# Attention, token and channel mixing and a gated block on one core: another planner, and channel mixing that adds six blocks at once

## The chip, the core and the metric

One core of a Trainium2 chip runs the program. The metric is device microseconds of one execution. TensorE is called PE here, VectorE DVE, ScalarE ACT, GpSimd POOL; SyncE (SP) issues the DMAs.

## What is computed

Batch 4, sequence 448, model width 768 (12 heads of 64), all float32:

```python
scores = q @ k.T / 8 ; scores[upper triangle] = -1e9
attn = exp(scores - max) ; attn /= sum(attn) + 1e-9
x = attn @ v                                    # heads side by side: 448 x 768 a batch
u = x + (relu(x.T @ w_tok1) @ w_tok2).T         # token mixing, 448 -> 256 -> 448
y = u + relu(u @ w_ch1) @ w_ch2                 # channel mixing, 768 -> 1536 -> 768
h = relu(y @ w_in) ; a, v = halves of h         # 512 wide each
vn = (v - mean(v)) / sqrt(var(v) + 1e-6)
out = (a * (w_spatial @ vn + b_spatial)) @ w_out
```

## The kernel before

**Products.** Each float32 operand is split into a rounded part and a rest, and a product is three matmuls (`mm3`, L336 to L338). The left operand of a matmul is 128 x 128, the right one up to 448 columns.

**Attention.** There are 24 pairs of heads (pair n is batch n // 6). A pair's scores (PE, bank `pss`, L497) are made in two jobs, one for the row blocks 3 and 0 and one for 2 and 1; they use 64 of PE's rows for each head. DVE masks them and takes the maximum (L506), ACT takes the exponential (L523), POOL normalises (L544), the result is transposed (PE, `pst`, L581; in the last pairs on DVE), and a weighted sum follows (PE, `pso`, L683 and L688), which uses 64 of PE's columns for each head. All other matmuls use the whole array.

**Token mixing** of half a batch (`psm`) transposes U, multiplies twice, and DVE adds the result to U (L787).

**Channel mixing** of batches 0 and 1 is `channel(b)`: 24 units of weights of 128 x 768, in the order of `UNITS` (L32 to L34). A unit (1, f) is hidden block f: 18 matmuls into a bank `ps1`, relu on ACT (L843) and its rest on DVE (L330) into `hid`. There are six buffers `h0` to `h5`. A unit (2, q, e) holds the weights from the hidden blocks 3q to 3q+2 to two output blocks: for each output block 9 matmuls into a bank `ps2`, and DVE adds the bank to U (L859). That is 48 additions in the two batches. The units come as three of the first kind, then three of the first and three of the second in turn. Both kinds take the PSUM banks 6 and 7. Batches 2 and 3 use products that need fewer multiplications (`channel_pair`, bank `psf`; L1001 and L1080 are DVE's sums), and then comes the gated block (`psv`, `psf`, `psp`).

**Weights** arrive as 64-bit words. `narrow` (L343 to L358) makes float32 of a piece of 384 columns in three DVE steps, each of which reads what the one before wrote in a PSUM bank `psw`:

```python
if k == 0:   # L351
    nc.vector.tensor_scalar(o, words(1), 3, 0x3FFFFFFF, op0=ALU.logical_shift_left, op1=ALU.bitwise_and)
elif k == 1: # L353
    nc.vector.scalar_tensor_tensor(o, words(1), 0xC0000000, o, op0=ALU.bitwise_and, op1=ALU.bitwise_or)
else:        # L355
    nc.vector.scalar_tensor_tensor(w().bitcast(U32), words(0), 29, o, op0=ALU.logical_shift_right, op1=ALU.bitwise_or)
```

A unit is loaded into one of the buffers `way` (768 KB, L381), converted in two pieces, stored in DRAM as `plain` (384 KB, L395) and loaded again as `whl` (L818), where ACT and POOL split it (L819, L820 by way of L327). `whl` has four buffers. The weights of the gated block go the same way as `gw`. Pieces of the first eight units use bank 7, all later ones bank 3.

**The order of the work** is made by a planner. All work is recorded as jobs with an engine, a duration, what they read and write, and a priority. `Plan.order` (L~135 to L~200) runs a list scheduler (`run`) that goes through a model of the engines: of the jobs that could start first on an engine (within 0.03) the one with the lowest priority number is taken. Then `due` works backwards through that plan and gives every job its latest start as its priority. That is done up to six times, and the plan that ends first in the model is written out as each engine's program. An engine works through its program in order. The names and lines that the prediction speaks of are those above.

Of the kernel before, what the change touches and what calls it, by code (L numbers as in the profile page):

```python
# [2 lines left out]

# [59 lines left out]
PASSES = 6  # L63
DUE = "ACT", "DVE", "POOL", "SP", "PE"
# [9 lines left out]


class Buf:


    def __init__(self, make, tag, prev=None, banks=None):
        self.make, self.tag, self.prev, self.banks = make, tag, prev, banks  # L80
        self.jobs, self.tile, self.left = [], None, 0

# [7 lines left out]
class Job:  # L90
    def __init__(self, eng, us, emit, prio, at, size, index, port, other):
        self.eng, self.us, self.emit, self.prio, self.at, self.size, self.index = eng, us, emit, prio, at, size, index
        self.other = other
        self.port = port or eng == "POOL"
        self.before, self.after, self.bufs = set(), [], set()


class Plan:
# [11 lines left out]
    def job(self, eng, us, emit, r=(), w=(), touch=(), prio=0.0, at=0.0, size=0, port=False, other=None):  # L110


        j = Job(eng, us, emit, prio, at, size, len(self.jobs), port, other)
# [16 lines left out]
        j.bufs |= set(touch)  # L130
        self.jobs.append(j)
        return j

    def order(self):
# [10 lines left out]
        own = {j: (j.eng, j.us, j.emit, j.prio) for j in self.jobs}  # L145
        best = None
        for k in range(PASSES):
            for j in self.jobs:
                j.eng, j.us, j.emit, _ = own[j]
            if not self.run():  # L150
                break
            end = max(j.start + j.us for j in self.jobs)
            if best is None or end < best[0]:
                best = end, [(j.start, j.eng, j.us, j.emit) for j in self.jobs], {b: b.tag for j in self.jobs for b in j.bufs if b.banks}
            self.due(end, own, k)
        for j, x in zip(self.jobs, best[1]):
            j.start, j.eng, j.us, j.emit = x
        for b, tag in best[2].items():
            b.tag = tag
        return sorted(self.jobs, key=lambda j: (j.start, j.index))  # L160

    def due(self, end, own, k):

        jobs = sorted(self.jobs, key=lambda j: (j.start, j.index))
        owners = {}
        for j in jobs:
            for b in j.bufs:
                if b.banks and b not in owners.setdefault(b.tag, []):
                    owners[b.tag].append(b)
        later = {}  # L170
# [3 lines left out]
        late, pe = {}, end  # L174
        for j in reversed(jobs):
            t = pe if j.eng == "PE" else end
            for a in j.after:
                lat = 0.0
                if a.eng != j.eng or j.eng == "SP":
                    lat = 0.25 if j.eng == "PE" else 0.1  # L180
                    if a.eng == "PE":
                        lat += 0.3 if j.start < START else 0.8
                if j.eng == "SP":
                    lat += j.size / 340e3 + LANDING
                t = min(t, late.get(a, end) - lat)
            for b in j.bufs:
                if j in b.jobs:
                    for a in later.get(b, ()):
                        t = min(t, late.get(a, end) - 0.3)
            late[j] = t - j.us  # L190
            if j.eng == "PE":
                pe = late[j]
        for j in self.jobs:
            if own[j][0] in DUE and own[j][3] < 1e8:
                j.prio = late[j]

    def run(self):
# [11 lines left out]
        dma = port_free = 0.0  # L209
        avail = {e: [] for e in engines}  # L210
        def add(j):
            for e in (j.eng, j.other[0]) if j.other else (j.eng,):
                avail[e].append(j)

# [4 lines left out]
        def start(j, e):  # L219
            s = max(free[e], j.ready, port_free if j.port else 0.0)  # L220
            for b in j.bufs:
                if b.banks and b.tag is None:
                    s = max(s, min(bank_free[i] for i in b.banks))
            return s

        done = 0
        while done < len(self.jobs):
            best = None
            for e in engines:
                if not avail[e]:  # L230
                    continue
                starts = [(start(j, e), j) for j in avail[e]]
                first = min(s for s, _ in starts)
                if first == inf:
                    continue
                s, j = min(((s, j) for s, j in starts if s <= first + 0.03), key=lambda x: (x[1].prio, x[1].index))
# [4 lines left out]
            s, j, e = best  # L241
            avail[j.eng].remove(j)
            if j.other:
                avail[j.other[0]].remove(j)
                if e != j.eng:
                    j.eng, j.us, j.emit = j.other
            for b in j.bufs:
                if b.banks and b.tag is None:
                    b.tag = min(b.banks, key=lambda i: (bank_free[i] > s, -bank_free[i] if bank_free[i] <= s else bank_free[i]))
                    bank_free[b.tag] = inf  # L250
            j.start = s
            free[j.eng] = s + j.us
            if j.port:
                port_free = s + j.us
            end = s + j.us
# [4 lines left out]
            for b in j.bufs:  # L260
                if j in b.jobs:
                    b.left -= 1
                    if b.left == 0 and b.banks:
# [1244 lines left out]
```

## Time and profile before

| | before |
|---|---|
| runs, us | 759.65 (759.39 to 760.97), median of 3 |
| profiled execution: span, us | 760.7 |
| profiled execution: own time, us | 760.97, the highest of the three, is the nearest to its span |
| PE busy, us | 747.2 |
| DVE busy, us | 622.3 |
| ACT busy, us | 427.4 |
| POOL busy, us | 298.2 |
| DMA, MB | 122.0 |

Times in rows are microseconds from the start of the span. "Busy" is the time in which an engine worked on an instruction. A row of the timeline has the start, the length, engine, line and operation, the output and input by their names, and in brackets how long the engine was idle before it and which instruction ended the wait. Matmuls overlap, so their starts are to be compared, not their lengths. PEclk is the clock that PE was granted, as a share of 2.4 GHz.

### The profile page before, as it was taken

The numbers are of one execution on the slowest core, as the hardware profiler recorded it, in microseconds if no ns is written. First come the engines' busy times: TensorE is split into PE (matmuls) and PEld (weight loads), VectorE is DVE, ScalarE is ACT, GpSimd is POOL, SyncE is SP. The second block draws the span as 40 slices with busy tenths as digits, with TensorE's granted clock in tenths as the row PEclk, the third lists the DMA queues.
The fourth block names the chain that finished last, engine by engine and source line by source line (L and its number), as shares of the span: only waits on it lengthen the run. The fifth ranks groups of instructions, "written<-read, shape, count | busy, mean of one in ns | idle before, by whom it ended". The sixth has DMA issues, their size and how long they took to land. (4 is left out here: it accounts for less than half of the span.)

```text
span 760.7 us, 12440 instructions
## 1 busy us (share of the span) xinstructions
PE 747.2 (98%) x4216; PEld 640.3 (84%) x4216; DVE 622.3 (82%) x1512; ACT 427.4 (56%) x1040; POOL 298.2 (39%) x354
## 2 busy tenths in 40 slices
PE   8999999999989999999999999999999999999998
PEld 4577778888887888888889989998988888888997
DVE  6999599999867878876469978999999897599482
ACT  6998776445347765552336666654573665545241
POOL 4788764265494766563310000000420151542210
PEclk9999999999999999999999999999999999999999
DMA  6687158999976898898823122520301100400213
GB/s 228 207 285 238 55 163 316 335 318 333 339 225 190 298 307 250 234 304 220 241 84 117 39 84 84 187 84 1 118 22 42 43 0 1 132 1 28 83 49 133
DMA packets 48608, 122.02 MB, mean 160 GB/s; under 512 B 4896, under 2 KB 20256, under 8 KB 48032
## 3 DMA queue, kind: packets, MB, share of 16 engines
q1 hardware_dynamic: 48544, 121.23, 48.7%
q8 instruction: 33, 0.54, 0.3%
q14 instruction: 31, 0.25, 0.1%
HBM read 91.46 MB, written 29.75 MB: 159 GB/s over the span
## 5 line engine op out<-in xcount | busy, mean ns | idle before, releaser
L336 PE MATMUL psf<-fb,fa 128*128 128x448 f32 x420 | 154.0, 367 | 1.2 <-DVE hs L1001 0.6
L337 PE MATMUL psf<-fb,fa 128*128 128x448 f32 x420 | 153.7, 366 | 0.0
L338 PE MATMUL psf<-fb,fa 128*128 128x448 f32 x420 | 153.6, 366 | 0.0
L327 POOL TENSOR_TENSOR whl<-whl 128x768 fp32r<-128x768 f32 x45 | 83.2, 1851 | 89.5 <-ACT whl L819 89.4
L523 ACT ACTIVATE P<-P,stats 128x448 f32<-128x448 f32 (+3 forms) x192 | 96.1, 505 | 31.1 <-DVE stats L506 30.8
L544 POOL TENSOR_SCALAR P<-P,stats 128x448 f32<-128x448 f32 (+3 forms) x192 | 88.3, 483 | 38.1 <-DVE stats L535 30.8
L336 PEld LDWEIGHTS psf<-fb,fa 128*128 128x128 f32 x420 | 78.9, 188 | 9.2 <-DVE hs L1001 1.0
L337 PEld LDWEIGHTS psf<-fb,fa 128*128 128x128 f32 x420 | 78.9, 188 | 6.8
L338 PEld LDWEIGHTS psf<-fb,fa 128*128 128x128 f32 x420 | 78.9, 188 | 6.7
L506 DVE CUSTOM_DVE_ANT_0 P<-pss,mask 128x448 f32<-128x448 f32 (+3 forms) x192 | 70.9, 415 | 16.4 <-PE pss L497 16.0
L938 ACT CAST fa<-raw 128x384 fp32r<-128x384 f32 (+1 forms) x112 | 56.4, 531 | 42.7 <-DVE raw L951 21.6
L327 POOL TENSOR_TENSOR wv<-wf,wv 128x512 fp32r<-128x512 f32 x6 | 9.2, 1546 | 153.2 <-ACT wv L1156 153.2
L327 DVE TENSOR_TENSOR fa<-raw,fa 128x384 fp32r<-128x384 f32 (+1 forms) x109 | 61.0, 585 | 7.1 <-ACT fa L938 7.1
L336 PE MATMUL ps<-hid,whl 128*128 128x448 f32 x144 | 55.2, 383 | 3.1 <-DVE hid L330 1.9
L819 ACT CAST whl<-whl 128x768 fp32r<-128x768 f32 x45 | 37.4, 833 | 34.6 <-DMA whl<-plain 33.5
L336 PE MATMUL ps<-uhl,whl 128*128 128x448 f32 x144 | 55.6, 386 | 0.2 <-DVE U L859 0.2
L338 PE MATMUL ps<-hid,whl 128*128 128x448 f32 x144 | 53.3, 370 | 0.0
L337 PE MATMUL ps<-hid,whl 128*128 128x448 f32 x144 | 53.3, 370 | 0.0
L338 PE MATMUL ps<-uhl,whl 128*128 128x448 f32 x144 | 52.7, 366 | 0.0
L337 PE MATMUL ps<-uhl,whl 128*128 128x448 f32 x144 | 52.7, 366 | 0.0
L859 DVE TENSOR_TENSOR U<-ps,U 128x448 f32<-128x448 f32 x48 | 29.5, 619 | 20.9 <-PE ps L338 20.8
L327 POOL TENSOR_TENSOR ql<-stage,qh 128x896 fp32r<-128x896 f32 x18 | 38.1, 2116 | 14.9 <-issue 11.7
(174 smaller groups left out, 1793.2 us busy)
## 6 DMA issues: line engine op xcount, KB each, us to landing
way<-in_wch SPq DMA_DIRECT2D x24, 768.0 KB, 5.7
whl<-plain SPq DMA_DIRECT2D x45, 384.0 KB, 5.0
stage<-in_qkv SPq DMA_DIRECT2D x23, 448.0 KB, 4.7
plain<-way SPq DMA_DIRECT2D x24, 384.0 KB, 6.7
raw<-plain SPq DMA_DIRECT2D x24, 384.0 KB, 3.9
round<-PB SPq DMA_DIRECT2D x7, 1024.0 KB, 6.2
PT<-round SPq DMA_DIRECT2D x28, 256.0 KB, 6.2
v<-in_qkv SPq DMA_DIRECT2D x24, 256.0 KB, 4.1
```

The lines of the kernel that those rows point to most:

```text
L327: e.tensor_tensor(lo, x, hi.bitcast(F32), op=ALU.subtract)
L336: nc.tensor.matmul(ps, ah, bh, start=(first and i == 0), stop=False, **kw)
L337: nc.tensor.matmul(ps, ah, bl, start=False, stop=False, **kw)
L338: nc.tensor.matmul(ps, al, bh, start=False, stop=(last and i == n - 1), **kw)
L506: nc.vector.tensor_tensor_reduce(out=P(i)[:M, j, :], in0=ps(i, j), in1=mask[:M, S - 128 : S - 128 + W] if j == 0 and n < BLOCKS or M == 64 ...
L523: nc.scalar.activation(P(i)[:M, j, :], P(i)[:M, j, :], AF.Exp, bias=s.t[:M, 0, c : c + 1], scale=-1.0, accum_out=s.t[:M, 1, c : c + 1])
L544: nc.gpsimd.tensor_scalar(P(i)[:M, j, :], P(i)[:M, j, :], s.t[:M, 2, c : c + 1], 1.0, op0=ALU.mult, op1=ALU.mult)
L819: job("ACT", act(DM, False), lambda: nc.scalar.copy(w.t[:, 0, :], w.t[:, 1, :].bitcast(F32)), r=ks, w=ks, prio=p)
L859: job("DVE", dve(S), lambda d=d, ps=ps: nc.vector.tensor_tensor(u.t[:, d, :], ps.t[:, :S], u.t[:, d, :], op=ALU.add), r=[(ps, 0), *u_keys( ...
L938: job("ACT", act(n, False), lambda: nc.scalar.copy(part(o, 0), at(d)), r=[key(d)], w=[wk], prio=p + 0.1 * o)
```

## The change

Three things change. First, the planner. A job has a `mode` (1 for the scores, which tile PE's rows, 2 for the weighted sums, which tile its columns, 0 for all else); in the model a change of mode costs `SWITCH`, and a job in another mode than the last one has its priority number raised by `STAY`. A DVE job that reads what a DVE job wrote starts `CHAIN` later than that one ends. Durations of DVE and of some PE jobs are other numbers. Priorities come from two rules, `late` (as before) and `justified` (which packs each engine backwards), up to eight passes each, and then from 300 random variations of the best plan's priorities; the plan that ends first in the model is kept. Second, the units of channel mixing come as six of the first kind, then six of the second, twice, and an output block of batches 0 and 1 sums six hidden blocks, that is two units, 18 matmuls, in one bank before DVE adds it to U: 24 additions (L938) instead of 48. Third, the pieces of the first eight units may use bank 7 or bank 3.

The core of the diff (renamed helpers, the backward pass of `justified` and the caching in `run` are left out):

```diff
-UNITS = [(1, f) for f in range(3)]
-for q in range(4):
-    UNITS += [(1, f) for f in range(3 * q + 3, min(3 * q + 6, NF))] + [(2, q, e) for e in range(3)]
+UNITS = []
+for x in range(2):
+    UNITS += [(1, f) for f in range(6 * x, 6 * x + 6)] + [(2, q, e) for e in range(3) for q in (2 * x, 2 * x + 1)]
...
-PASSES = 6
+PASSES, TRIALS = 8, 300
+SWITCH, STAY, NEAR = 0.105, 3.0, 0.03
+CHAIN = 0.115
...
+        for rule in (self.late, self.justified):
+            prios = [j.own[3] for j in self.jobs]
+            for _ in range(PASSES):
+                if not self.attempt(prios):
+                    break
+                prios = rule(self.end)
+        dice = Random(1)
+        for _ in range(TRIALS):
+            spread, share = dice.choice((0.3, 1.0, 3.0)), dice.choice((0.02, 0.1, 0.5))
+            lo = dice.uniform(-50.0, 450.0) if dice.random() < 0.5 else None
+            hi = None if lo is None else lo + dice.choice((10.0, 30.0, 100.0))
+            prios = [p + dice.gauss(0.0, spread) if p < 1e7 and (lo is None or lo <= p < hi) and dice.random() < share else p for p in self.best[1]]
+            self.attempt(prios)
...
+            if e == "PE":
+                s, j = min(((s, j) for s, j in starts if s <= first + NEAR), key=lambda x: (x[1].prio + (x[1].mode != mode) * STAY, x[1].index))
+                return s + (j.mode != mode) * SWITCH, j
...
-        return (n * 1.05 + 60) / 1e3 if psum else (n * 1.09 + 40) / 1e3
+        return (n * 1.042 + 68) / 1e3
...
-            job("DVE", (n * 1.03 + 165) / 1e3, lambda k=k: step(k), r=[dk, (ps, 0)] if k else [dk], w=[wk] if k == 2 else [(ps, 0)], touch=[wk[0]], prio=prio)
+            job("DVE", (n * 1.04 + 70) / 1e3, lambda k=k: step(k), r=[dk, (ps, 0)] if k else [dk], w=[wk] if k == 2 else [(ps, 0)], touch=[wk[0]], prio=prio)
...
-        convert(i % 3 if i < 6 else 1 + i % 2, wch[:, i * DM : i * DM + DM], parts, LOW + i, (7,) if i < 8 else (3,), keep=i)
+        convert(i % 3 if i < 6 else 1 + i % 2, wch[:, i * DM : i * DM + DM], parts, LOW + i, (7, 3) if i < 8 else (3,), keep=i)
...
     def ch2(b, q, e, i):
-        w = WU[b, i]
+        w = [WU[b, i - 1], WU[b, i]]
         u = U[b]
-        hs = [hidden[b, 3 * q + f] for f in range(3)]
         for dd in range(2):
             d = 2 * e + dd
             ps = bank(banks_c, "ps2")
+            for x in range(2):
+                hs = [hidden[b, 3 * (q - 1 + x) + f] for f in range(3)]
+
+                def mms(dd=dd, ps=ps, x=x, hs=hs):
+                    cs = [slice(HALF * dd + 128 * f, HALF * dd + 128 * f + 128) for f in range(3)]
+                    mm3(ps.t[:, :S], [(w[x].t[:, 0, c], w[x].t[:, 1, c], h.t[:, 0, :], h.t[:, 1, :]) for c, h in zip(cs, hs)], first=x == 0, last=x == 1)
+
+                job("PE", 1.82, mms, ...)
             job("DVE", dve(S), lambda d=d, ps=ps: nc.vector.tensor_tensor(u.t[:, d, :], ps.t[:, :S], u.t[:, d, :], op=ALU.add), ...)
...
             if u[0] == 1:
                 ch1(b, u[1], i, xs)
-            else:
+            elif u[1] % 2:
                 ch2(b, u[1], u[2], i)
```

Every matmul of the program before is in the changed one. How the order moves is shown at three places. DVE in the channel mixing of batch 0, before: `psw` and `way` or `gw` rows are conversions, a `U` row is the addition of an output block.

```order
L859 TENSOR_TENSOR U_317<-ps_2478,U_317 128x448
L351 TENSOR_SCALAR psw<-gw 128x384
L353 SCALAR_TENSOR_TENSOR psw<-gw,psw 128x384
L355 SCALAR_TENSOR_TENSOR gw<-gw,psw 128x384
L859 TENSOR_TENSOR U_317<-ps_2500,U_317 128x448
L351 TENSOR_SCALAR psw<-way_156 128x384
L353 SCALAR_TENSOR_TENSOR psw<-way_156,psw 128x384
L355 SCALAR_TENSOR_TENSOR way_156<-way_156,psw 128x384
L859 TENSOR_TENSOR U_317<-ps_2519,U_317 128x448
```

The same place in the changed program:

```order
L429 TENSOR_SCALAR psw<-way_158 128x384
L938 TENSOR_TENSOR U_331<-ps_1580,U_331 128x448
L431 SCALAR_TENSOR_TENSOR psw<-way_158,psw 128x384
L433 SCALAR_TENSOR_TENSOR way_158<-way_158,psw 128x384
L938 TENSOR_TENSOR U_331<-ps_1620,U_331 128x448
L429 TENSOR_SCALAR psw<-way_158 128x384
L431 SCALAR_TENSOR_TENSOR psw<-way_158,psw 128x384
L433 SCALAR_TENSOR_TENSOR way_158<-way_158,psw 128x384
L429 TENSOR_SCALAR psw<-way_154 128x384
L431 SCALAR_TENSOR_TENSOR psw<-way_154,psw 128x384
L433 SCALAR_TENSOR_TENSOR way_154<-way_154,psw 128x384
```

Before, each addition had one piece's conversion ahead of it; now there are steps of up to three pieces between two additions, and an addition may stand between two steps of a piece.

PE in the early pairs, before: `pss` rows are scores, `pso` rows weighted sums, `psm` and `pst` rows use the whole array.

```order
L497 MATMUL pss<-ql,qh 64x64 x2
L497 MATMUL pss<-qh,ql 64x64 x2
L741 MATMUL psm<-ident,U_317 64x128 x3
L683 MATMUL pso<-PT,v 64x448 x2
L688 MATMUL pso<-PT,v 64x384 x2
L688 MATMUL pso<-PT,v 64x256 x2
L688 MATMUL pso<-PT,v 64x128 x2
L741 MATMUL psm<-ident,U_317 128x128 x3
L497 MATMUL pss<-qh 128x320 x2
L497 MATMUL pss<-ql,qh 128x320 x2
```

Pairs of the same batch in the changed program:

```order
L766 MATMUL pso<-PT,v 64x256 x2
L766 MATMUL pso<-PT,v 64x128 x2
L575 MATMUL pss<-qh 128x448 x2
L575 MATMUL pss<-ql,qh 128x448 x2
L575 MATMUL pss<-qh,ql 128x448 x2
L575 MATMUL pss<-qh 64x64 x2
L575 MATMUL pss<-ql,qh 64x64 x2
L575 MATMUL pss<-qh,ql 64x64 x2
L575 MATMUL pss<-qh 128x320 x2
L575 MATMUL pss<-ql,qh 128x320 x2
L575 MATMUL pss<-qh,ql 128x320 x2
```

Before, the two jobs of a pair's scores had whole-array work and a weighted sum between them; now they follow each other and the weighted sum directly. Counted over the whole program, PE goes from one of the three kinds to another 121 times before and 99 times now.

DVE at the start, before: `stats` and `P` rows are the reductions of the first pairs, `way` is a weight of token mixing.

```order
L534 TENSOR_SCALAR stats_65<-stats_65 128x4
L535 RECIPROCAL stats_65<-stats_65 128x4
L506 ISA P_208,stats_66<-pss,mask 128x448
L506 ISA stats_66 128x1
L534 TENSOR_SCALAR stats_65<-stats_65 128x4
L535 RECIPROCAL stats_65<-stats_65 128x4
L506 ISA P_208,stats_66<-pss,mask 128x448
```

The same place in the changed program:

```order
L612 TENSOR_SCALAR stats_65<-stats_65 128x4
L613 RECIPROCAL stats_65<-stats_65 128x4
L429 TENSOR_SCALAR psw<-way_152 128x384
L584 ISA P_211,stats_66<-pss,mask 128x448
L584 ISA stats_66 128x1
L612 TENSOR_SCALAR stats_65<-stats_65 128x4
L613 RECIPROCAL stats_65<-stats_65 128x4
L584 ISA P_211,stats_66<-pss,mask 128x320
```

The first step of the first conversion, which before came after all reductions of pair 1, now stands ahead of them.

## Rows read from the trace of the kernel before

**Rows 1.** The page's first part: busy time, share of the span, instructions of each engine.

```profile
PE 747.2 (98%) x4216; PEld 640.3 (84%) x4216; DVE 622.3 (82%) x1512; ACT 427.4 (56%) x1040; POOL 298.2 (39%) x354
```

**Rows 2.** Stretches of 20 us: busy time of each engine, PE's clock, DMA share, GB/s.

```profile
40.00:60.00 20.00, 19.93 (x154) 15.87 (x151) 19.01 (x51) 18.22 (x54) 18.06 (x29) 1.00 0.85 268
...
140.00:160.00 20.00, 20.00 (x115) 17.16 (x114) 19.15 (x41) 6.59 (x12) 5.54 (x3) 1.00 1.00 354
180.00:200.00 20.00, 18.68 (x96) 16.02 (x95) 18.39 (x44) 7.69 (x18) 8.07 (x7) 1.00 0.94 332
200.00:220.00 20.00, 18.07 (x84) 16.28 (x83) 14.49 (x31) 10.55 (x19) 14.90 (x15) 0.91 0.85 287
```

**Rows 3.** PE's waits: line, releaser, us in total, times, longest.

```profile
PE ps L336 <- DVE hid L330: 1.9, 1, 1.9
PE ps L336 <- DVE U L859: 1.2, 2, 1.1
PE psp L1355 <- DVE gate L1363: 0.9, 2, 0.7
PE psf L336 <- DVE hs L1001: 0.6, 1, 0.6
PE psf L336 <- DVE U L1080: 0.6, 1, 0.6
```

**Rows 4.** PE's timeline where a weighted sum follows channel mixing.

```profile
99.60 0.36 PE L337 MATMUL ps<-uhl,whl 128*128 128x448 f32 x1
99.80 0.37 PE L338 MATMUL ps<-uhl,whl 128*128 128x448 f32 x1
100.10 0.97 PE L683 MATMUL pso<-PT,v 128*64 128x448 f32 x4
```

**Rows 5.** PE's timeline around two waits in batch 0's channel mixing.

```profile
194.91 0.47 PE L336 MATMUL ps<-hid,whl 128*128 128x448 f32 x1 [1.05 <-DVE U L859]
...
209.82 0.37 PE L338 MATMUL ps<-hid,whl 128*128 128x448 f32 x1
212.13 0.47 PE L336 MATMUL ps<-hid,whl 128*128 128x448 f32 x1 [1.94 <-DVE hid L330]
212.43 0.36 PE L337 MATMUL ps<-hid,whl 128*128 128x448 f32 x1
```

**Rows 6.** DVE's timeline in the same stretch.

```profile
194.24 0.62 DVE L859 TENSOR_TENSOR U<-ps,U 128x448 f32<-128x448 f32 x1
194.77 0.55 DVE L351 TENSOR_SCALAR psw<-way 128x384 uint32<-128x384 uint32 x1
195.36 0.56 DVE L353 SCALAR_TENSOR_TENSOR psw<-way,psw 128x384 uint32<-128x384 uint32 x1
195.96 0.55 DVE L355 SCALAR_TENSOR_TENSOR way<-way,psw 128x384 uint32<-128x384 uint32 x1
196.43 0.62 DVE L859 TENSOR_TENSOR U<-ps,U 128x448 f32<-128x448 f32 x1
...
210.98 0.56 DVE L355 SCALAR_TENSOR_TENSOR way<-way,psw 128x384 uint32<-128x384 uint32 x1 [0.75 <-DMA plain<-way]
```

**Rows 7.** The loads of channel units and the conversions' last steps: ns min/median/max, first and last start.

```profile
L381 SPq DMA_DIRECT2D way<-in_wch x24: 327/332/857, 18.6 to 200.9; - x24
...
L355 DVE SCALAR_TENSOR_TENSOR way<-way,psw x50: 377/553/564, 30.5 to 213.2; 128x384 uint32<-128x384 uint32 x48, 128x224 uint32<-128x224 uint32 x2
```

**Rows 8.** DMA issues: KB each, us to landing.

```profile
whl<-plain SPq DMA_DIRECT2D x45, 384.0 KB, 5.0
```

**Rows 9.** The start: SP's first weight loads with their landing, and a DVE row.

```profile
3.52 1.66 SPq L381 DMA_DIRECT2D way<-in_wtok  x3
...
way<-in_wtok SPq DMA_DIRECT2D x1, 768.0 KB, 6.5
...
9.44 0.62 DVE L506 CUSTOM_DVE_ANT_0 P<-pss,mask 128x448 f32<-128x448 f32 x1 [0.36 <-PE pss L497]
```

**Rows 10.** GB/s that the DMA engines moved in the first 16 us, in 40 slices.

```profile
GB/s 0 0 0 0 73 242 364 197 108 116 155 294 367 405 389 398 425 399 343 435 428 388 392 428 436 383 393 425 412 394 430 421 430 394 233 99 18 0 0 0
```

More of the change, by code (lines that the diff above doesn't have):

```diff
@@ L73 @@
 BLOCKS = 17
+SWITCH, STAY, NEAR = 0.105, 3.0, 0.03
+CHAIN = 0.115
+NUMBER = count()
 class Buf:
@@ L144, in order @@
                 p.after.append(j)
[L145 to L155, printed above, removed]
@@ L157, in order, with attempt @@
             j.start, j.eng, j.us, j.emit = x
-        for b, tag in best[2].items():
+        for b, tag in self.best[3].items():
             b.tag = tag
         return sorted(self.jobs, key=lambda j: (j.start, j.index))
[L162 to L168, printed above, removed]
+    def attempt(self, prios):
+        for j, p in zip(self.jobs, prios):
+            j.eng, j.us, j.emit, _ = j.own
+            j.prio = p
+        if not self.run():
+            return False
+        self.end = max(j.start + j.us for j in self.jobs)
+        if self.best is None or self.end < self.best[0]:
+            self.best = self.end, prios, [(j.start, j.eng, j.us, j.emit) for j in self.jobs], {b: b.tag for j in self.jobs for b in j.banked}
+        return True
@@ new lines, in lag, with next_in_bank @@
+    def lag(self, j, a):
+        lat = CHAIN if j.eng == a.eng == "DVE" else 0.0
+        if a.eng != j.eng or j.eng == "SP":
+            lat = 0.25 if j.eng == "PE" else 0.1
+            if a.eng == "PE":
+                lat += 0.3 if j.start < START else 0.8
+        if j.eng == "SP":
+            lat += j.size / 340e3 + LANDING
+        return lat
+    def next_in_bank(self):
+        owners, later = {}, {}
+        for j in sorted(self.jobs, key=lambda j: (j.start, j.index)):
+            for b in j.banked:
+                if b not in owners.setdefault(b.tag, []):
@@ L209, in run @@
         dma = port_free = 0.0
+        mode = 0
         avail = {e: [] for e in engines}
+        found, stale = {}, set(engines)
         def add(j):
@@ L217, in run, with look @@
                 add(j)
[L219 to L224, printed above, removed]
+        def look(e):
+            f, starts, first = free[e], [], inf
+            for j in avail[e]:
+                s = j.ready if j.ready > f else f
+                if j.port and port_free > s:
+                    s = port_free
+                for b in j.banked:
+                    if b.tag is None:
+                        k = sum(c.tag is None and c.banks == b.banks for c in j.banked)
+                        s = max(s, sorted(bank_free[i] for i in b.banks)[k - 1])
+                starts.append((s, j))
+                if s < first:
+                    first = s
+            if first == inf:
+                return None
+            if e == "PE":
+                s, j = min(((s, j) for s, j in starts if s <= first + NEAR), key=lambda x: (x[1].prio + (x[1].mode != mode) * STAY, x[1].index))
+                return s + (j.mode != mode) * SWITCH, j
+            return min(((s, j) for s, j in starts if s <= first + NEAR), key=lambda x: (x[1].prio, x[1].index))
         done = 0
@@ L229, in run @@
             for e in engines:
-                if not avail[e]:
+                if e in stale:
+                    found[e] = look(e)
+                if found[e] is None:
                     continue
[L232 to L236, printed above, removed]
+                s, j = found[e]
                 if best is None or (s, j.prio) < (best[0] - 0.1, best[1].prio) or s < best[0] + 0.1 and j.prio < best[1].prio:
@@ L254, in run @@
                 port_free = s + j.us
+                stale.update(("DVE", "POOL"))
             end = s + j.us
@@ L259, in run @@
             done += 1
[L260 to L263, printed above, removed]
-                        bank_free[b.tag] = end + 0.3
+            for b in j.of:
+                b.left -= 1
+                if b.left == 0 and b.banks:
+                    bank_free[b.tag] = end + 0.3
+                    stale.update(("PE", "DVE", "ACT"))
             for a in j.after:
-                lat = 0.0
+                lat = CHAIN if j.eng == a.eng == "DVE" else 0.0
                 if a.eng != j.eng or j.eng == "SP":
```

111 lines of the change are left out of this document (67 added, 44 removed).

## The prediction

> **What bounds the kernel now.** I read the page's shares of busy time first. PE works for 747.2 of 760.7 us [rows 1], so almost all of the time is PE's own work, and the changed kernel has the same matmuls. A gain must come from the 13.5 us in which PE stands idle, or from work that only the order causes. DVE has 622.3 us [rows 1], which leaves it room over the whole span; but an average hides stages. So the stretches come second: between 180 and 220 PE is busy for 18.68 and 18.07 of 20 us, and in the second of them its granted clock falls to 0.91 of full [rows 2]. No other stretch of 20 us has both. PE's waits come third: two of the largest lie there (1.9 us for `hid`, 1.2 us for the addition to U), and 0.9, 0.6 and 0.6 us lie in the products after 400 us [rows 3].
>
> The timelines say why PE waits in the first place. From one addition to the next DVE takes 196.43 - 194.24 = 2.19 us [rows 6]: one addition (0.53) and one piece of a conversion (0.59 + 0.60 + 0.47). PE makes the 9 matmuls of an output block in 9 x 0.20 = 1.83 us (0.20 is the step from 99.60 to 99.80 [rows 4]). So for that stretch **DVE is the bound**, by 0.36 us per output block, until PE has used up its banks and waits. At 210 us DVE in turn waits 0.75 us for a store of converted words [rows 6], and PE stands 1.94 us [rows 5].
>
> **The change, part by part.**
>
> *Switches of PE's tiling.* From a matmul of channel mixing to a weighted sum the step is 0.30 us (99.80 to 100.10) where the step before it is 0.20 [rows 4]; a switch costs some 0.094 us. The new order has 99 instead of 121: 22 x 0.094 = **-2.1 us**. Bounds: -1.0, if half of them fell beside a wait, and -2.3.
>
> *Half as many additions in channel mixing.* 24 additions of 0.53 us [rows 6] leave DVE, 12.8 us. PE now makes 18 matmuls, 3.66 us, per addition; an addition and two pieces take DVE 0.53 + 2 x 1.66 = 3.85 us, or 3.4 where the pieces are interleaved (below). So DVE stops being the bound there, and by the new order most conversions are done before the second group of units. The loss now is worked out so: PE idle 1.32 + 1.93 us [rows 2], a clock of 0.91 for 20 us, 1.8 us, and three waits [rows 3] whose true cost exceeds the shown idle time by 0.27 us each (209.82 to 212.13 to 212.43 is 2.61 us, two steps would be 0.40; 2.61 - 0.40 - 1.94 [rows 5]). Together 5.9 us. I keep 0.5 for what remains: **-5.4 us** (bounds -5.9 and 0).
>
> *A second bank, and spacings that the planner knows.* A DVE step that reads what the step ahead wrote starts 0.59 or 0.60 us after it; one that doesn't, 0.47 us (195.96 to 196.43) [rows 6]. Two conversions interleaved save 0.12 us a step. I count about 60 such steps in the new order, 7 us of DVE work, none of it on PE's path by itself. [...]
>
> *Six hidden blocks at once.* An output block needs two units and all six `hid` buffers. The ring of four `whl` buffers thus holds two pairs. Where channel mixing runs undisturbed, a buffer is free after 5.5 us of its pair's 7.3 us and needed at 14.6 us: 9.1 us for a load of 5.0 us [rows 8] and the split by ACT and POOL behind it, some 2.7 us. Before it was three units, 11 us. I cost it at nothing; the cover is 1.4 us, and if a load takes longer than 6.4 us, each pair stops PE for the excess. Attention work between the units adds to the cover in batch 0. A reload waits in SP's queue until its buffer is free, and behind it wait the loads of units and operands, which is how a late buffer would reach DVE.
>
> *The waits after 400 us.* The program there is nearly the same; the new order puts single gating groups between products that followed each other. The four waits there (for `gate`, `hs` and U) show 0.9 + 0.6 + 0.6 = 2.1 us [rows 3], and with 0.27 for each 3.2 us. I take half: **-1.7 us** (0 to -3.2).
>
> *The start.* The first conversion step now stands ahead of pair 1's reductions. Its words are asked for at 3.52 us and take 6.5 us, so they land at 10.0; the reductions behind it began at 9.44 [rows 9]. DVE stands up to 0.6 us, and exponentials and transposes of pair 1 behind it. More of DVE's work also comes early. I take **+1.0 us** (0 to +2).
>
> *Loads.* The changed kernel converts earlier. Counting in DVE's new order with the spacings of these shapes, 143 us of work stand ahead of the last step of a channel unit, 182 before, where that step ran at 213.2 [rows 7]: DVE was 31 us behind its own work. With 6 us of lag (the start) the last step falls at 149. By the same count PE starts to wait longer than now where that step comes later than 161. SP's queue must until then move 24 units in and out (28 MB), 17 reloads (7 MB) and operands of ten pairs (9 MB), 44 MB from 18.6 us on. At the 268 GB/s of 40 to 60 [rows 2], 11 MB are through by 60; the other 33 MB take 93 us at 354 GB/s (140 to 160, all DMA engines busy [rows 2]) and end at 153. That is inside 161. The planner's model charges all loads at 340 GB/s in one queue, so an order that asks for more had no advantage in it. For waits here and there I add **+1.0 us** (0 to the rivals below).
>
> Sum: -2.1 - 5.4 - 1.7 + 1.0 + 1.0 = -7.2 us, from the profiled execution's 760.97 to 753.8. The median of the runs, 759.65, is 1.3 us below that execution, so the forecast is **752.5 us**.
>
> **The rivals.**
>
> *A: loads set the pace, a little.* At 332 GB/s (180 to 200 [rows 2]) the 33 MB take 99 us and end at 159: no loss. If the early stretch moves less, say 7 MB by 60, 37 MB take 111 us and end at 171, 10 us past 161. The order is fixed, so PE can't draw other work ahead; but not every unit comes that late, and the last ones stand behind attention. I take half, +5 us: 757.5. For it: full DMA engines at 354 GB/s in the densest stretch. Against: the start moved 388 to 436 GB/s over many slices [rows 10], and DVE waited for words only late. The Trainium skill ("DMA: Bandwidth & Descriptors", section "Where 436 GB/s comes from") gives 435 GB/s for the ports and some 358 for HBM transfers, and has the lower one bind. The densest stretch agrees with it, the start doesn't; by 358 the end is estimated at 152, by 420 at 139, and both lie inside 161.
>
> *B: only the switches are gained.* PE's stalls move instead of going: the six-block sums need the last `hid` directly, and the waits after 400 come back at other places. Then -2.1 of the switches and some +1 of the start remain: 758.5 us. For it: DVE stays at over 90% of many stretches. Against: the stretch with the largest loss had its cause in 2.19 against 1.83 us, and that ratio is gone.
>
> *C: slower, by late conversions.* If the 33 MB move at 287 GB/s (200 to 220, DMA share 0.85 [rows 2]), as loads do when each waits for its buffer `way` until the store of converted words has landed, they take 115 us and end at 175, 14 us past 161. PE stands for all of it, and each stand may lower its clock as at 213 us: 752.5 + 14 = 766.5 us. It is slower than before from the point where the last step falls after some 170 us, or below 300 GB/s. For it: before, DVE was 31 us behind at this step; if that lag stays, the step comes at 174. Against: much of that lag was planned, as DVE waited for PE, not for words.
>
> *D: the ring of four.* If each load takes 1 us longer than its cover, 12 pairs stand 1 us each: +12 us, 764.5. For it only the narrow 1.4 us; I count it with C.
>
> **How the numbers follow.** Forecast (749 to 756): 0.57. A (756 to 758): 0.17. B (758 to 761): 0.12. C and D: 0.12. Above the forecast's own gain, PE waits gone everywhere (below 749): 0.02. A measurement of this kernel can tell 0.2%, 1.5 us, from no change. Faster, then, is the forecast, A, the tail and a sixth of B, 0.78; same is most of B, 0.10; slower C and D, 0.12. The range holds the forecast with its bounds (the switches at -2.3, the stalls at -5.9 and after 400 at -3.2, the start at 0 give -11.4 + 0, so 748) and A and half of B: 747.5 to 759.5.
>
> **What would show it.** Right: PE busy falls by about 2 us (switches) and its idle time by 4 to 6; no stretch between 100 and 240 has PE below 19.5 of 20 us or a clock below 1.00; the additions come 24 times at the same 0.53 us step; the last conversion of a channel unit starts between 149 and 161 us; DMA shows over 330 GB/s from 60 to 150. A: PE waits for `whl` or `hid` between 100 and 170, with DVE idle for DMA `way`. B: the same PE idle time in other rows. C: the last conversion after 170. D: PE or its weight load waits for POOL's `whl` in batch 1's channel mixing, evenly spaced by 7.3 us. The forecast is wrong altogether if PE's busy time rises, or if its steps inside a stage are no longer 0.20 us.

## The result and the profile after

The changed kernel is slower: 768.86 us (765.94 to 769.90, 4 runs) against 759.66 us (759.39 to 760.97), a ratio of 1.0117 with a 95% interval of 1.0092 to 1.0141. The forecast was 752.5 us with a range to 759.5. The two profiled executions show only a part of that: the one of the changed kernel is the quickest of its four (765.94 us, a span of 764.2 us, a mean granted clock of 1.000; the others have spans of 766.4 to 768.1 us and clocks of 0.994 to 0.997), and the one of the kernel before, with a span of 760.7 us and a clock of 0.997, is a slow one (81 of its 89 later executions have a shorter span, median 758.5 us). So the rows below show the smaller part of the loss, 3.5 us of span. In every run on record the time is 1.7 to 2.1 us above the span; a span of 760.7 us thus belongs to a time of some 762.5 us, which none of the three runs in the table of before has.

The stretches of the changed kernel (busy time of each engine, PE's clock, DMA share, GB/s), which answer to [rows 2]:

```profile
0.00:20.00 20.00, 17.92 (x98) 9.63 (x98) 14.15 (x64) 14.88 (x49) 9.28 (x30) 1.00 0.75 272
20.00:40.00 20.00, 18.80 (x144) 11.99 (x144) 19.86 (x77) 19.40 (x69) 17.52 (x33) 1.00 0.58 189
40.00:60.00 20.00, 17.51 (x128) 13.77 (x125) 19.68 (x57) 16.12 (x46) 14.81 (x20) 1.00 0.62 204
60.00:80.00 20.00, 17.36 (x123) 14.17 (x122) 18.43 (x53) 13.69 (x37) 14.63 (x21) 1.00 0.84 276
80.00:100.00 20.00, 19.48 (x130) 15.73 (x129) 16.94 (x44) 10.71 (x29) 9.60 (x14) 1.00 0.90 294
100.00:120.00 20.00, 19.74 (x119) 16.82 (x117) 17.35 (x39) 10.69 (x23) 7.38 (x5) 1.00 0.91 314
120.00:140.00 20.00, 19.52 (x95) 17.34 (x94) 16.41 (x32) 3.37 (x5) 5.52 (x3) 1.00 0.88 280
140.00:160.00 20.00, 19.33 (x114) 16.87 (x114) 17.68 (x42) 9.84 (x22) 14.38 (x14) 1.00 0.97 349
...
180.00:200.00 20.00, 20.00 (x148) 16.82 (x147) 15.62 (x52) 15.94 (x42) 17.61 (x27) 1.00 0.69 208
200.00:220.00 20.00, 19.00 (x138) 16.14 (x137) 14.86 (x40) 13.12 (x37) 17.50 (x19) 1.00 0.66 200
...
240.00:260.00 20.00, 18.14 (x148) 13.96 (x148) 15.64 (x49) 16.22 (x47) 16.81 (x23) 1.00 0.80 265
```

The place that the prediction spoke of is mended: PE has 20.00 and 19.00 us between 180 and 220 where it had 18.68 and 18.07, and the clock is 1.00. But PE now stands 6.3 us between 20 and 80, and 1.9 us between 240 and 260. Over 20 to 80 as a whole, before and after:

```profile
20.00:80.00 60.00, 58.33 (x449) 42.00 (x446) 55.70 (x201) 56.74 (x176) 50.10 (x81) 1.00 0.71 231
```

```profile
20.00:80.00 60.00, 53.67 (x389) 39.93 (x388) 57.97 (x186) 49.21 (x149) 46.96 (x72) 1.00 0.68 223
```

PE's busy time there is 4.7 us less, while DVE is busy for 58 of 60 us. Who holds PE (its waits in the changed kernel: total, times, longest), to be read beside [rows 3]:

```profile
PE psm L819 <- DVE xs L405: 3.8, 3, 1.4
PE pst L659 <- DVE PT L662: 3.2, 3, 1.9
...
PE psp L1434 <- DVE gate L1442: 1.2, 1, 1.2
PE ps L414 <- DVE U L938: 1.1, 2, 0.6
...
PE ps L414 <- DVE hid L408: 0.5, 1, 0.5
```

The waits of channel mixing (`ps`) have shrunk from 3.1 to 1.6 us, those after 400 us from 2.1 to 1.2. New are 7 us at the transposes of attention and token mixing (`pst`, `psm`): their PSUM bank is free only when DVE has copied it (`PT`) or taken the rest from it (`xs`). DVE is late with these. Its waits for DMAs, in the kernel before and in the changed one:

```profile
DVE psw L351 <- DMA gw<-in_wgv: 2.7, 5, 1.1
DVE psw L351 <- DMA way<-in_wch: 1.5, 2, 1.1
DVE way L355 <- DMA plain<-way: 0.7, 1, 0.7
```

```profile
DVE psw L429 <- DMA way<-in_wch: 10.0, 13, 1.9
...
DVE psw L429 <- DMA gw<-in_wgv: 8.4, 5, 2.7
```

18.4 us for words that had not landed, where it was 4.2. And one small step on DVE takes twice as long as before (DVE's lines, before and after; the second line of the latter is the addition, half as often as in the kernel before):

```profile
L534 DVE TENSOR_SCALAR stats<-stats 128x8 f32<-128x8 f32 (+1 forms) x25 | 7.7, 310 | 2.3 <-ACT P L523 2.2
```

```profile
L612 DVE TENSOR_SCALAR stats<-stats 128x8 f32<-128x8 f32 (+1 forms) x25 | 14.8, 593 | 2.2 <-ACT P L601 1.8
L938 DVE TENSOR_TENSOR U<-ps,U 128x448 f32<-128x448 f32 x24 | 14.8, 617 | 16.4 <-PE ps L416 16.4
```

The timeline of the changed kernel shows how either reaches PE:

```profile
41.34 1.82 DVE L612 TENSOR_SCALAR stats<-stats 128x8 f32<-128x8 f32 x1
...
44.45 1.13 DVE L405 TENSOR_TENSOR xs<-psm,xs 128x384 fp32r<-128x384 f32 x2
...
41.01 2.12 POOL L405 TENSOR_TENSOR ql<-stage,qh 128x896 fp32r<-128x896 f32 x1 [0.99 <-POOL P L537]
...
45.06 0.55 PE L819 MATMUL psm<-ident,U 128*128 128x128 f32 x3 [1.42 <-DVE xs L405]
...
245.39 0.69 DVE L429 TENSOR_SCALAR psw<-gw 128x512 uint32<-128x512 uint32 x1 [2.30 <-DMA gw<-in_wgv]
...
247.46 1.04 DVE L612 TENSOR_SCALAR stats<-stats 128x8 f32<-128x8 f32 x1
...
248.65 0.57 DVE L662 COPY PT<-pst 128x448 f32<-128x448 f32 x1
...
249.28 0.66 PE L659 MATMUL pst<-ident,P 128*128 128x128 f32 x4 [1.86 <-DVE PT L662]
```

At 41.34 the addition of 1e-9 to eight sums starts on DVE and ends at 43.16; POOL's `ql` ends at 41.01 + 2.12 = 43.13. Behind the addition stands all of DVE's queue, `xs` with it, and PE waits 1.42 us. Of the 25 additions 11 take more than 0.3 us, and each of these ends some 0.03 us after a `tensor_tensor` of POOL that had started before it; in the kernel before, 5 of 25 do. At 245 a conversion stands 2.30 us for its words; behind it the addition takes 1.04 us, again to the end of a `ql` of POOL; behind both stands the copy `PT`, and PE waits 1.86 us. Two theories came from this. **W**: the new order asks for words with no time to spare, and where they are late, DVE's queue stands. **P**: DVE's addition and POOL's large operations exclude each other, and the new order lets them meet more often. Rivals were that DVE has simply too much to do early (D), that the channel mixing in groups of six costs by itself (M), and, later, that one draw of the random search was unlucky (L).

### The profile page after: what moved, and what is told of

It reads as the page before. It is cut to its first block, busy times and chain, and to the rows that moved or that the text cites. A ratio compares the mean times of both kernels' runs of the same rounds, so it can differ in the third digit from the quotient of the medians.

```text
span 764.2 us, 12406 instructions
## 1 busy us (share of the span) xinstructions
PE 746.0 (98%) x4216; PEld 640.0 (84%) x4216; DVE 613.5 (80%) x1492; ACT 427.4 (56%) x1036; POOL 289.9 (38%) x354
## 5 line engine op out<-in xcount | busy, mean ns | idle before, releaser
L405 DVE TENSOR_TENSOR fa<-raw,fa 128x384 fp32r<-128x384 f32 (+1 forms) x109 | 59.4, 568 | 13.0 <-ACT fa L1017 12.8
L659 PE MATMUL pst<-ident,P 128*128 128x128 f32 x272 | 38.4, 277 | 4.0 <-DVE PT L662 3.2
```

The costliest lines, as they stand in the source:

```text
L405: e.tensor_tensor(lo, x, hi.bitcast(F32), op=ALU.subtract)
L659: nc.tensor.transpose(ps.t[:, c : c + 128], src, ident)
```

## The experiments

Each ratio is to the kernel before, timed on the same chip. The changed kernel itself was timed only once, in the four runs above; "by the ratios" compares ratios that were measured at different times.

### Words that land sooner, in an order that is kept

Both edits leave the planner's input as it is, so the order of the changed kernel stays (the traces have DVE's, ACT's and POOL's instructions in the same sequence). `half_words`:

```diff
-nc.sync.dma_start(b.t[:, : 2 * n], src.bitcast(U32))
+m = n if keep is None else n // 2
+nc.sync.dma_start(b.t[:, : 2 * m], src[:, :m].bitcast(U32))
...
+d0 = c0 if keep is None else c0 % HALF
+narrow(lambda c0=d0, c1=d0 + c1 - c0: b.t[:, 2 * c0 : 2 * c1], ...)
```

> The changed kernel with its order kept, but only half of each channel unit's words are loaded (384 KB instead of 768; the second piece converts the first piece's words again, so half the weights are left out). Theory W (words late: the new order asks for each unit's words with no time to spare, DVE stands in front of a conversion until they land, and PE behind it): DVE's waits for the words of channel units fall from 10.0 us to under 3, the last conversion step moves from 170.5 to 163 or earlier, and the time falls by 4 to 8 us, to 761 to 765. Rival D (DVE's work itself stands in the wrong order early on, loads play no part): those waits vanish too, but PE still waits 5 us or more between 20 and 80 us and the time stays at 767 to 770.

763.56 us, ratio 1.0046 (1.0029 to 1.0062). DVE's waits for channel units are gone from the list, the last conversion step falls at 166.3. As W had it in time, not quite in place (163).

`two_loads`:

```diff
-nc.sync.dma_start(b.t[:, : 2 * n], src.bitcast(U32))
+for k in range(1 if keep is None else 2):
+    m = n if keep is None else HALF
+    nc.sync.dma_start(b.t[:, 2*m*k : 2*m*k + 2*m], src[:, m*k : m*k + m].bitcast(U32))
```

> The changed kernel with its order kept, each channel unit's words loaded by two DMAs of 384 KB, so that the first piece's words land earlier. Theory W: DVE waits less for the first piece, 10.0 us becomes 4 to 8, and the time falls by 1 to 4 us, to 765 to 768. Rival D: no change, 768 to 770. If the DMA engines themselves are full (rival B, bandwidth), no change either, and the second piece waits for as long as the first did.

761.17 us, ratio 1.0025 (1.0006 to 1.0043): by the ratios 7 us less than the changed kernel, more than W had expected. DVE's waits in it:

```profile
DVE psw L429 <- DMA gw<-in_wgv: 4.9, 4, 2.3
DVE way L433 <- DMA plain<-way: 2.9, 4, 1.6
DVE psw L429 <- DMA way<-in_wch: 1.8, 2, 1.4
```

The bytes are the same, and between 80 and 140 us they now move at 313 to 326 GB/s, where it was 280 to 314; so it isn't the DMA engines' rate that had held DVE. Between 20 and 80 us PE still stands 5.5 us: W explains the later stands, not the early ones.

### The addition that waits for POOL

`no_add`, in the order of the changed kernel:

```diff
-nc.vector.tensor_scalar_add(s.t[:, 2, cols], s.t[:, 1, cols], 1e-9)
-nc.vector.reciprocal(s.t[:, 2, cols], s.t[:, 2, cols])
+nc.vector.reciprocal(s.t[:, 2, cols], s.t[:, 1, cols])
```

> The changed kernel with its order kept, but the step that adds 1e-9 to the sums of the softmax (a tensor_scalar of 8 columns on DVE, 25 times) is left out; the reciprocal reads the sums themselves. In the changed kernel that step takes 14.8 us in all, up to 1.84 us once, and ends when a tensor_tensor of POOL ends. Theory P (DVE and POOL get in each other's way at this step, and all of DVE's queue stands behind it): the excess of some 10 us leaves DVE, the waits of PE between 20 and 80 us fall by 2 us or more, and the time is 762 to 767. Theory W alone (late words): 767 to 769.5. If the reciprocal now waits in its place, its mean rises from 201 ns to over 400 and the time stays.

760.80 us, ratio 1.0014 (0.9998 to 1.0030), by the ratios nearly 8 us less; P had expected 762 at best. The reciprocal doesn't take over the wait:

```profile
L612 DVE RECIPROCAL stats<-stats 128x8 f32<-128x8 f32 (+1 forms) x25 | 4.8, 194 | 1.8 <-ACT P L601 1.3
```

Eight of these 25 run wholly beside a `tensor_tensor` of POOL, and none takes more than 0.21 us. PE stands 3.5 us between 20 and 80, 2.9 less than in the changed kernel, though DVE's waits for the words of channel units are no shorter (11.1 us). And the stall at 245 is gone; DVE and POOL at that place, and the stretch:

```profile
241.97 0.69 DVE L429 TENSOR_SCALAR psw<-gw 128x512 uint32<-128x512 uint32 x1 [1.77 <-DMA gw<-in_wgv]
...
244.04 0.19 DVE L612 RECIPROCAL stats<-stats 128x8 f32<-128x8 f32 x1
...
243.61 2.11 POOL L405 TENSOR_TENSOR ql<-stage,qh 128x896 fp32r<-128x896 f32 x1 [0.85 <-POOL ql L405]
...
240.00:260.00 20.00, 19.95 (x158) 16.66 (x155) 14.94 (x52) 17.35 (x49) 18.52 (x25) 1.00 0.81 276
```

PE's idle time by stretches, in the changed kernel, in `two_loads` and in `no_add`: between 80 and 180 us 1.9, 0.1 and 2.2 us; between 180 and 260 us 2.9, 0.7 and 0.1 us. So P's part lies mostly before 80 us, W's between 80 and 180, and after that either of these two edits takes most of the stall away: late words and the addition stand one behind the other in DVE's queue there. (In `half_words` the stall at 245 stays, 1.8 us between 240 and 260.) That the gains of 7 and 8 us don't add up in the next run fits this.

`both` and `before_both` make both edits, in the changed kernel and in the kernel before.

> The changed kernel with its order kept, each channel unit loaded by two DMAs as in two_loads, and without the addition of 1e-9. Theories W and P together: 755 to 759, PE idle for under 4 us between 20 and 80 us. W alone: as two_loads, 760.5 to 762. Rival D (DVE has too much to do early, whatever it waits for): over 760.

757.54 us, ratio 0.9970 (0.9960 to 0.9981).

> The kernel before with the same two edits, as a control. If the words and the addition cost the order of before little, as its waits suggest (2.2 us for words and stores, 3.5 us over the usual length at the addition, against 10.0 and 10.5 in the changed kernel), it gains 0 to 3 us: 757 to 760.5. If they cost every order alike, it gains as much as the changed kernel does, 8 us or more: 752 or less.

757.96 us, ratio 0.9968 (0.9949 to 0.9987). The edits give the order of before 0.3% and the changed order 1.5%: the latter had been the one that paid for late words and for the addition. With both edits, the two kernels can't be told apart. That is the answer to where the forecast gain is: in the order as it was planned, and with these two costs taken away, the change is worth nothing that can be told from zero. (The words of the gated block, which the edit leaves alone, still keep DVE waiting 9.3 us in `both`, 3.4 us in `before_both`.) PE between 20 and 80 us, in `both` and then in `before_both`:

```profile
20.00:80.00 60.00, 57.24 (x414) 43.28 (x413) 57.92 (x187) 50.84 (x155) 50.86 (x76) 1.00 0.73 238
```

```profile
20.00:80.00 60.00, 58.61 (x450) 42.74 (x449) 54.15 (x194) 57.02 (x177) 50.88 (x81) 1.00 0.67 224
```

The changed order still loses 1.4 us there, and DVE, which it fills early with conversions, has 3.8 us more to do in that stretch.

### Planner or channel mixing

`planner_only` is the changed kernel with `UNITS`, `ch2` and the one bank of before; `mixing_only` is the kernel before with the new `UNITS`, `ch2` and two banks. `planner_both` and `mixing_both` add the two edits above.

> The changed planner alone: the units of channel mixing, the 9-matmul output blocks, the 48 additions and the one conversion bank are as before. Theory W: the planner's closer costs are what left no room, so DVE waits for words here too (over 5 us) and the time is 760 to 768, no faster than before. Rival M (the channel mixing in groups of six is what costs, by the ring of four weight buffers and the late last hidden block): the time is 751 to 757.

760.73 us, ratio 1.0008 (0.9988 to 1.0028): no change. DVE waits 3.2 us for words of channel units, less than the 5 that W had expected.

> The planner of before with the new channel mixing (six blocks an addition, 24 additions) and the second conversion bank. Theory W: DVE's waits for words stay under 5 us; the channel mixing by itself is worth little either way, 756 to 765. Rival M: 766 to 772, with PE waiting for hidden blocks, additions or weights in channel mixing of batches 0 and 1.

772.21 us, ratio 1.0156 (1.0139 to 1.0174), the slowest of all, at the end of M's range in time, and not as M had it in place. PE stands 7.8 us between 20 and 80, and DVE waits only 1.6 us for words of channel units (6.9 us for those of the gated block):

```profile
20.00:80.00 60.00, 52.21 (x378) 37.20 (x378) 56.83 (x188) 50.57 (x153) 47.17 (x74) 0.97 0.67 228
```

> The changed planner with the channel mixing of before, and the same two edits. It waited for words 3.2 us and its addition took 4.5 us over the usual length. Theories W and P: it gains 2 to 5 us, 755 to 759. If the new channel mixing is worth its 12.8 us of DVE work once the words come in time, the kernel called both is faster than this one; if not, this one is the fastest of the four.

757.30 us, ratio 0.9968 (0.9952 to 0.9984), as `both` and `before_both`.

> The kernel called mixing_only (the planner of before, six hidden blocks an addition, the second bank) with two loads a unit and without the addition of 1e-9. Rival M (the mixing in groups of six costs by itself): it stays 8 us or more above before_both's 758.0, at 766 or more. W and P (it lost by late words and the addition, as the changed kernel did): 757 to 762.

767.67 us, ratio 1.0111 (1.0047 to 1.0175). Here W and P fail: under the planner of before, the new mixing is slow for another reason, most of which lies in the first 80 us (PE stands 9.3 us there, 6.1 more than in `before_both`; the span is 10.7 us longer). Why that order comes out worse there, no run here shows.

### A planner that expects later landings, and other draws

`landing_only` changes one number of the changed kernel:

```diff
-LANDING = 2.3
+LANDING = 3.3
```

> The changed kernel with one number of its planner: a transfer counts as landed 3.3 us after its bytes have gone through the queue, not 2.3. Nothing else; the order is planned anew. Theory W (the order has no room for words that land later than the planner assumed): DVE's waits for the words of channel units fall from 10.0 us to under 6 and the time to 758 to 765. If the time is over 766, a planner that knows of later landings doesn't help and W doesn't explain the loss of the whole change.

759.21 us, ratio 0.9973 (0.9956 to 0.9990). One number takes the loss away; but the order is planned anew, so this is another draw of the random search as well. DVE's waits for DMAs in it:

```profile
DVE psw L429 <- DMA way<-in_wch: 4.0, 5, 1.5
DVE psw L429 <- DMA gw<-in_wgv: 1.0, 2, 0.7
```

Other draws of the search, `dice_2` (`Random(2)`, landings at 2.3), `dice_2_later` and `dice_3_later` (seeds 2 and 3, landings at 3.3):

> The changed kernel with another seed for its 300 random variations (2 instead of 1), landings at 2.3 as in the change. Theory W is a property of the planner, so another draw loses as well: DVE waits for words over 5 us, 763 to 770. Rival L (luck: the change's slow order is one unlucky draw): 752 to 760.

762.79 us, ratio 1.0031 (1.0010 to 1.0052). Slower than before again, but by the ratios 6.5 us less so, between the ranges of W and L. Its waits are no shorter:

```profile
DVE psw L429 <- DMA way<-in_wch: 12.9, 9, 2.2
...
DVE psw L429 <- DMA gw<-in_wgv: 4.0, 3, 2.0
```

> Seed 2 with landings at 3.3 us. W: faster than dice_2 by 3 us or more, DVE waits for words under 6 us, 754 to 763. L: no order between the two, within 3 us of each other or the other way round.

760.47 us, ratio 1.0002 (0.9981 to 1.0023): 2.3 us under `dice_2`, with 2.5 us of waits for channel units; short of the 3 us that W asked, and within the 3 us that L allowed.

> Seed 3 with landings at 3.3 us, a third draw of what landing_only is. W: within 4 us of landing_only's 759.2. L: 764 or more is as likely as not.

762.04 us, ratio 1.0024 (1.0006 to 1.0042), by the ratios 3.9 us above `landing_only`, with 4.3 us of waits. So both W and L hold in part: in both draws the planner with 2.3 leaves DVE 10 to 13 us of waits for channel units, in all three with 3.3 it leaves 2.5 to 4.3; and the draw moves the time by some 4 to 6.5 us besides. The 768.9 us of the change are W, P and an unlucky draw together; how much each has of them, these runs don't tell.

`later_36` and `later_32` are `both` planned anew, with landings at 3.6 or 3.2 us and 0.22 us for the reciprocal's job; `later_three_36` is the first of them with the mixing and bank of before.

> The kernel called both (two loads a unit, no addition of 1e-9) planned anew with 3.6 us for a landing and 0.22 us for the reciprocal's job. W: the order leaves room, DVE waits for words under 2 us, PE stands under 3 us between 20 and 80 us; 749 to 755, the fastest yet. If the order's own length decides, it is no faster than both: 757 or more.

754.76 us, ratio 0.9912 (0.9888 to 0.9936): the fastest kernel of this study, under both the kernel before and the change. Its stretches:

```profile
20.00:40.00 20.00, 19.19 (x146) 12.09 (x145) 19.69 (x74) 19.25 (x66) 15.33 (x31) 1.00 0.64 196
40.00:60.00 20.00, 19.39 (x156) 16.03 (x154) 19.93 (x66) 17.43 (x51) 17.81 (x25) 1.00 0.82 290
60.00:80.00 20.00, 19.04 (x153) 14.88 (x150) 18.71 (x61) 18.49 (x54) 18.61 (x28) 1.00 0.75 253
```

DVE no longer waits for channel units at all, the last of their conversions falls at 190.4, 20 us later than in the changed kernel, and between 80 and 400 us PE never stands. By the ratios this is 6.7 us under the kernel before, about the size of the forecast gain, and 4.4 us under `both`. No run plans the kernel before anew with 3.6 us, so how much of it the new planner has brought, and how much the number, is not shown.

> As later_36 with 3.2 us. W: 749 to 756; by how much the two differ shows how far the search's luck goes.

754.85 us, ratio 0.9927 (0.9898 to 0.9955), the same.

> later_36 with the channel mixing and the conversion bank of before (three blocks an addition). If the six-block additions are worth something once words come in time, it is slower than later_36's 754.8 by 2 us or more (757 to 762); if they are worth nothing, 753 to 756.

755.68 us, ratio 0.9938 (0.9914 to 0.9961). By the ratios the six-block additions, 12.8 us less work on DVE, are worth 2 us here; the two intervals overlap, so this can't be told from zero.

## Why the prediction was wrong

**What held.** The stall of the stretch from 180 to 220 went: PE's idle time there fell from 3.25 to 1.00 us, and the clock stayed at 1.00. But the 5.4 us of this term were priced from one execution in which the clock had fallen to 0.91, 1.8 us of the term; 75 of the 89 later executions of the kernel before have a mean clock of 0.999 or 1.000, so part of the term was not there to be gained. (Nor is it the only stretch with idle time and a lower clock: 740 to 760 us has PE at 17.11 of 20 us and a clock of 0.98.) The additions came 24 times at 617 ns. The waits after 400 us fell from 2.1 to 1.2 us shown and from four to one, about the 1.7 us of the forecast with 0.27 for each. Tiling switches: PE's busy time fell by 1.2 us, where these and the mended clock together should have given 3.9; by the prediction's own reckoning each new stand of PE hides 0.27 us in the busy time, so these can't be told apart here. The count of switches isn't exact either: 24 of the transposes of token mixing, counted as whole-array work, use 64 columns.

**The step that failed first: the loads.** The prediction put the last conversion at 149 us, held that it costs nothing up to 161, and worked out by rates (354 GB/s) that the loads are through by 153; so it added only 1.0 us. The last conversion came at 170.5, and DVE waited for words of channel units 13 times, 10.0 us. DVE's last conversion steps, and SP's waits ahead of the loads:

```profile
L433 DVE SCALAR_TENSOR_TENSOR way<-way,psw x53: 370/550/556, 20.2 to 170.5; 128x384 uint32<-128x384 uint32 x48, 128x224 uint32<-128x224 uint32 x4, 128x256 uint32<-128x256 uint32 x1
...
SPq L459 <- DVE way L433: 56.3, 22, 5.0
```

Two things in it were wrong. First, the time of the last conversion is not what costs: in `half_words`, in the same order, it comes at 166.3, past the 161, and PE stands 0.1 us between 80 and 180 us; in `later_36` it comes at 190.4. What costs is that a conversion which waits for its words holds all of DVE's queue behind it. Second, the loads are not a stream that runs at a rate. From the seventh unit on there are two buffers `way` (the expression `1 + i % 2`), and a load is issued when DVE has done the last step of the unit that was in its buffer. A load takes 6.4 us to land in this kernel (median, from the table of DMA issues; 5.7 in the kernel before) and the conversion of two pieces some 3.3 us, so two buffers allow a unit every (6.4 + 3.3) / 2 = 4.9 us (an estimate from these rows). The last 17 loads come 5.4 us apart on average, and 5.2 us apart in `half_words`, where a load lands after 3.9 us. So the order of DVE's work sets the pace and not the ring; but the ring leaves it only half a microsecond a unit, and a load that lands later than that makes DVE wait. `two_loads` moved the same bytes and cut these waits from 10.0 to 1.8 us. The DMA rate never reached 354 GB/s between 60 and 160 us (276 to 349): the prediction's argument was one of rates, and what the runs show to have mattered is the time until the words of one unit are there. Rival C came nearest. It gave 766.5 us for a last step after 170, and named the buffer `way`; but it had the loads wait for the store of the converted words, where they wait for DVE, and it let PE stand on late units, where PE in fact stood mostly at transposes, behind DVE's queue.

That the planner charges loads at 340 GB/s was read as a safeguard. It was none: by that rate and the 2.3 us that it adds, a load of 768 KB alone lands after 4.6 us in the model, where it took 6.4. With 3.3 in place of 2.3, all three draws leave DVE less to wait (2.5 to 4.3 us, against 10.0 and 12.9). The planner of before had the same 2.3, and left DVE only 1.5 us of these waits; that a search over 300 plans finds the ones which use up such an assumption fits this, but no run with fewer plans shows it.

**The second step: the start.** It was put at +1.0 us, at most +2, for one conversion step that waits for its words; the DVE work that comes early was named and given no price of its own. The step itself cost nothing: it ran at 8.91 us, and PE works 17.92 of the first 20 us, where it was 17.63. Between 20 and 80 us PE lost 4.7. `no_add` names the cause of 2.9 of them: the addition of 1e-9, which waits for POOL; it took part in the stall at 245 as well. The row was there to be read in the trace of before, 25 additions of eight columns at a mean of 310 ns, nearly twice the 166 ns of the median one; the prediction didn't look at it. The Trainium skill ("GPSIMD Engine Reference", section "1. Specifications") says that POOL shares its SBUF interfaces with VectorE, and that VectorE's instructions in a two-port mode or with two SBUF inputs contend with it. The trace fits that, with a price: 1.82 us for 0.17 us of work, to the end of POOL's instruction; that the addition runs in such a mode, no run shows. The reciprocal, in the same place in `no_add`, never takes more than 0.21 us.

**What it comes to.** Each in its own order, with the words in halves and without the addition, the changed kernel is at 0.9970 and the kernel before at 0.9968. So of the forecast -7.2 us nothing remains in that order beyond what the same two edits give the kernel before. They also mend the stretch that the change was to mend: PE's idle time between 180 and 260 us is 0.4 us in `before_both`, 3.3 in the profile of before. Only an order planned anew for later landings is faster than both.

**Left open.** Why the new mixing costs some 10 us under the planner of before. How much of the change's own order is luck: by the ratios four other draws lie 6.5 to 11 us below it, three of them with later landings as well. What the kernel before would gain if it were planned anew with later landings. And what the second bank and the price of a switch in the model are worth by themselves.

## What to carry to other kernels

A planner that searches many orders can find ones that lean on what its model leaves out; its model needs the time in which a transfer lands under load, and the operations of two engines that exclude each other. In a program whose engines work in order, look for what stands ahead of the instruction that PE needs: a cheap one (a conversion that nobody waits for, an addition to eight numbers) can hold the rest. Hold the round trip of a ring of two buffers, landing and use, against the pace at which the order uses it, and not only bytes against a rate; two smaller loads in place of a large one may be all that it needs.

## What was not expected of the hardware

An operation of DVE over eight columns from SBUF to SBUF took 1.82 us, until POOL's `tensor_tensor` ended; a reciprocal of the same eight columns took 194 ns on average and 205 at most in `no_add`, eight times beside the same POOL work. Half the transfer is not half the time: 768 KB landed 6.4 us after their issue (median), 384 KB after 5.5 where two such loads follow each other (`two_loads`), and after 3.9 where there is only one (`half_words`). So the gain of the two loads is, as far as these rows tell, that the first half's conversion can start while the second is on its way.
